# Attention and FFN in one kernel: one key transpose for each pair of heads, and the order of the cast loads

## The chip, the cores and the metric

The kernel runs on one core of a Trainium2 chip. The metric is the device time of one execution in microseconds, the median of several runs. The engines are PE (matmul; its weight loads are listed apart as PEld), DVE (vector), ACT (activations), POOL (general purpose) and SP (here only a queue that issues DMAs). They work side by side, each in the order of its own queue, and wait for each other on semaphores. DMAs run on 16 DMA engines which all queues share.

## The reference

Attention with queries pooled by two, for 8 batches of 8 heads of 1,152 positions of 64 values, then a feed-forward part without an activation function:

```python
q_pool = q.reshape(B, H, S // 2, 2, D).mean(axis=3)          # 576 queries a head
scores = np.matmul(q_pool, k.transpose(0, 1, 3, 2)) / np.sqrt(D)
attn = np.exp(scores - np.max(scores, axis=-1, keepdims=True))
attn = attn / (np.sum(attn, axis=-1, keepdims=True) + 1e-09)
attn_out = np.matmul(attn, v)
x = attn_out.transpose(0, 2, 1, 3).reshape(B * S // 2, H * D)   # 4608 x 512
out = ((x @ w1) * (x @ w2) @ w3) @ w_out
```

Inputs and output are float32. The kernel works in float16 with sums in float32, and multiplies w3 and w_out into one matrix first.

## The kernel before

**Tiles.** Two heads of one batch make a *pair*; there are 32 pairs (P = 0 to 31), and four of them make a batch. Of a pair, q, k and v are loaded by POOL-issued DMAs that cast float32 to float16 on the way, into `qst` (shared by an even and the next odd pair, 2 buffers), `kst` and `vst` (4 buffers each). The keys are needed transposed (`kT`, 64 values of two heads on 128 partitions, 9 blocks of 128 keys), and so are the pooled queries (`qT`).

**Two ways of transposing.** Pairs 0 to 7 are transposed on PE. From pair 8 on, `prep_dma(P)` does two pairs in one round. On POOL it adds neighbouring queries (`pool_q`, L122) and copies the keys of each pair from `kst` into `kc`, heads side by side (L142). On SP it issues a DMA transpose of the keys of both pairs, 18 blocks in one instruction (L145), and one of the pooled queries of both, 9 blocks (L148). There is one `kc` buffer for two pairs, and two of `kT` and of `qT`, again for two pairs each.

**The round's end.** Straight after `prep_dma`, `settled` (L152) has POOL copy one element of `kT`, so that POOL stands until the key transpose has landed. Then `load_two` (L106) issues six cast loads for the two pairs after: q, q, v, v, k, k. POOL does nothing else in this part of the program, so its instructions form one serial chain: q add, two key copies, the wait, six loads, and again. There are 12 rounds (pairs 8, 10, ... 30); the last one issues no loads.

**The main loop** (L576) has 108 iterations of three score chunks of 512 columns each. `scores` (L292) multiplies `kT` with `qT` on PE, `expo` (L302) takes the exponential on ACT into a ring, `attend` (L317) multiplies with V (`vt`, copied from `vst` on DVE, L135), and `normalize` divides on DVE and sends the result through DMA transposes on SP into `xT` (L342, L345). FFN units of 512 tokens (L411, L429) are put between these on PE once their batch is there. The loop is written out by hand (`manual_schedule`): each engine's queue has the order in which the program names the instructions. `prep_dma(P)` stands where the scores have reached 1.95 pairs ahead of pair P, but POOL isn't paced by that place: it runs as its own waits let it.

**Waits around the change.** A key transpose waits until PE has done the scores of the two pairs that held its `kT` buffer (for the round of pair P, pairs P-4 and P-3). A V load waits for the DVE copy out of its `vst` buffer. SP's queue also holds the `xT` transposes and the output writes (L450), in the program's order.

Of the kernel before, what the change touches and what calls it, by code (L numbers as in the profile page):

```python
# [23 lines left out]
def kernel(  # L24
# [11 lines left out]
    nc = tc.nc  # L36
# [38 lines left out]
    kst, vst, qst, kT, qT, kTs, qTs, qps = {}, {}, {}, {}, {}, {}, {}, {}  # L75

    def load_q(P):
        b, h0 = P // 4, 2 * (P % 4)
        if P % 2 == 0 or P == 1:
            qst[P // 2] = stage.tile([128, 2, 18, D], FP16, tag="qst", bufs=2, name="qst")  # L80
        o = 64 * (P % 2)
        nc.gpsimd.dma_start(
            out=qst[P // 2][o:o + 64].rearrange("p u t d -> p u (t d)"),
            in_=q[b, h0:h0 + 2].rearrange("u (p t) d -> p u (t d)", t=18))

    def load_k(P):
        b, h0 = P // 4, 2 * (P % 4)
        kst[P] = stage.tile([128, 2, NJ, D], FP16, tag="kst", name="kst")
        nc.gpsimd.dma_start(  # L89
            out=kst[P].rearrange("p u j d -> p u (j d)"),  # L90
            in_=k[b, h0:h0 + 2].rearrange("u (p j) d -> p u (j d)", j=NJ))

    def load_v(P):
        b, h0 = P // 4, 2 * (P % 4)
        vst[P] = stage.tile([128, 2, NJ, D], FP16, tag="vst", name="vst")
        nc.gpsimd.dma_start(  # L96
            out=vst[P].rearrange("p u j d -> p u (j d)"),
            in_=v[b, h0:h0 + 2].rearrange("u (p j) d -> p u (j d)", j=NJ))
# [7 lines left out]
    def load_two(P):  # L106
        load_q(P)
        load_q(P + 1)
        load_v(P)
        load_v(P + 1)  # L110
        load_k(P)
        load_k(P + 1)

    def pool_q(P, n=1):

        eng = nc.gpsimd if n == 2 else nc.vector
        pp, o = P // 2, 64 * (P % 2)
        if P % 2 == 0 or P == 1:
            qps[pp] = ab.tile([128, NJ, 2, D], FP16, tag="qp", bufs=2, name="qp")
        r = slice(o, o + 64 * n)  # L120
        src = qst[pp][r].rearrange("p u (c two) d -> p u c two d", two=2)
        eng.tensor_tensor(  # L122
            out=qps[pp][r].rearrange("p c u d -> p u c d"),
            in0=src[:, :, :, 0, :], in1=src[:, :, :, 1, :], op=ALU.add)

    def new_kq(P):
        if P % 2 == 0:
            kTs[P // 2] = ab.tile([128, 2, NJ, 128], FP16, tag="kT", bufs=2, name="kT")
            qTs[P // 2] = ab.tile([128, NJ, 128], FP16, tag="qT", bufs=2, name="qT")
        o = 64 * (P % 2)  # L130
        kT[P] = kTs[P // 2][:, P % 2]
        qT[P] = qTs[P // 2][:, :, o:o + 64]
# [4 lines left out]
    def prep_dma(P):  # L137

        pool_q(P, 2)
        for p in (P, P + 1):  # L140
            new_kq(p)
            nc.gpsimd.tensor_copy(  # L142
                out=new_kc(p).rearrange("p j u d -> p u j d").bitcast(mybir.dt.int32),
                in_=kst.pop(p).bitcast(mybir.dt.int32))
        nc.sync.dma_start_transpose(  # L145
            out=kTs[P // 2].rearrange("p t j f -> p (t j) f"),
            in_=kc2[P // 2].rearrange("p t j u d -> p (t j u d)"))
        nc.sync.dma_start_transpose(  # L148
            out=qTs[P // 2], in_=qps[P // 2].rearrange("p c u d -> p (c u d)"))

    def settled(P):
        nc.gpsimd.tensor_copy(out=seen, in_=kT[P][0:1, 0, 0:1])  # L152
# [1 line left out]
    kcs, kc2 = {}, {}  # L154

    def new_kc(P):
        if P % 2 == 0:
            kc2[P // 2] = ab.tile([128, 2, NJ, 2, D], FP16, tag="kc", bufs=1, name="kc")
        kcs[P] = kc2[P // 2][:, P % 2]
        return kcs[P]  # L160
# [241 lines left out]
    def ffn_groups(t):  # L402
# [70 lines left out]
        out=ident, in_=ident, compare_op=ALU.not_equal, fill=1.0,  # L473
# [102 lines left out]
    for it in range(NIT):  # L576
# [23 lines left out]
        if prepped < NPE:  # L600
            if it >= first_it(prepped) - (1 if prepped < 5 else 2):
                queue[0:0] = prep_groups(prepped)
                prepped += 1
                urgent = True
        elif prepped < NP and at >= prepped - 1.95:
            prep_dma(prepped)
            if loaded < NP:
                settled(prepped)
                load_two(loaded)
                loaded += 2  # L610
            prepped += 2
# [65 lines left out]
```

## Time and profile before

| what | value |
|---|---|
| median of 5 runs | 422.16 us |
| the five runs | 418.27, 420.03, 422.16, 423.85, 425.68 us |
| the profiled execution (one of the five) | 418.27 us |
| its span in the trace | 416.5 us |
| mean granted PE clock | 1.00 |
| POOL's queue (loads that cast) | 32.97 MB, 51.1% of 16 DMA engines |
| SP's queue (transposes, output) | 25.84 MB, 33.4% of 16 DMA engines |
| key transpose L145 | 12 times, 2.69 us of SP each, landing after 4.7 us (median) |
| query transpose L148 | 12 times, 1.37 us of SP each, landing after 4.3 us (median) |
| loads to landing (median): q, V, k | 6.4, 9.3, 11.4 us |

The span is what the trace covers; the profiled execution's own time is 1.8 us longer. A busy share is an average over the whole span. A line of a timeline has start, duration, engine, line of the kernel, the operation with what it writes and reads, and in brackets the idle time before it and what ended it. A line of the waits names who waited for whom, then the total, the number of times and the longest, in us.

### The profile page before, as it was taken

The page shows a single profiled execution, that of the slowest core. Times are in us where ns is not written, and L with a number is a line of the kernel's source. Part 1 is how long each engine was busy: PE and PEld are TensorE (multiplying, and loading weights), DVE is VectorE, ACT ScalarE, POOL GpSimd, SP SyncE. Part 2 cuts the span into 40 slices and gives each one's busy share as a digit, 9 for nine tenths or more (in the row PEclk, how much of TensorE's full clock was granted, in tenths as well). Part 3 has the DMA queues.
Part 4 walks back from the last instruction along what each step waited for, and adds up shares of the span by engine and source line. Part 5 has one row for each costly group of instructions (what it writes and reads, how often), then busy time and mean ns, then how long its engine had stood idle before and what let it go on. Part 6 is the DMA issues. An engine that isn't in the chain of part 4 may idle for free.

```text
span 416.5 us, 12709 instructions
## 1 busy us (share of the span) xinstructions
PE 406.3 (98%) x5507; PEld 271.7 (65%) x5507; DVE 195.7 (47%) x407; ACT 326.8 (78%) x357; POOL 121.0 (29%) x161
## 2 busy tenths in 40 slices
PE   8899999999999999999999999999999999999996
PEld 6677787766776577666865686667665876544443
DVE  2456655464445553555455534544455434614140
ACT  5999989989888889988888899898888889133332
POOL 6443331343435243434233161615252000000000
PEclk9999999999999999999999999999999999999999
DMA  8999999599989999997989998999898641050404
GB/s 185 204 200 193 192 205 203 104 171 136 175 154 207 141 149 168 168 170 132 164 131 210 120 175 165 181 130 162 174 186 145 97 90 22 10 117 2 102 2 102
DMA packets 95801, 59.76 MB, mean 143 GB/s; under 512 B 65152, under 2 KB 86144, under 8 KB 95744
## 3 DMA queue, kind: packets, MB, share of 16 engines
q0 software_dynamic: 26928, 32.97, 51.1%
q1 hardware_dynamic: 68656, 25.84, 33.4%
q8 instruction: 43, 0.70, 0.7%
q10 hardware_dynamic: 160, 0.13, 0.1%
q14 instruction: 14, 0.11, 0.1%
HBM read 67.11 MB, written 9.44 MB: 184 GB/s over the span
## 4 chain that ended last, share of the span: by engine, by line
PE 84%; DMA 10%; ACT 2%; POOL 1%; DVE 1%; issue 1%; SPq 0%; ACTq 0%; POOLq 0%
PE po L317 19%; PE psc L292 17%; PE pa L411 16%; PE pb L411 15%; PE pp L429 15%; DMA qst<-in_q_dram 7%; DMA xT<-in_moe_w_out_dram 3%; ACT er L302 2%; PE pT L395 2%; DMA out_dram<-osb 1%; DMA er<-in_k_dram 1%; POOL kst L89 0%; POOL w3h L356 0%; POOL vst L96 0%; DVE qp L122 0%
## 5 line engine op out<-in xcount | busy, mean ns | idle before, releaser
L302 ACT ACTIVATE er<-psc 128x1024 f16<-128x1024 f32 x324 | 307.4, 1029 | 39.7 <-PE psc L292 39.6
L317 PEld LDWEIGHTS <-er 128*128 128x128 f16 x2880 | 103.3, 97 | 22.0 <-issue 5.9
L317 PE MATMUL po<-vt,er 128*128 128x65 f16 x2880 | 110.3, 193 | 0.0
L292 PE MATMUL psc<-qT,kT 64*128 64x512 f16 (+7 forms) x1152 | 94.9, 285 | 3.0 <-ACT er L302 2.3
L423 DVE TENSOR_TENSOR gT<-pb,asb 128x512 f16<-128x512 f32 x72 | 49.8, 692 | 56.1 <-PE pb L411 55.4
L411 PE MATMUL pa<-xT,w1sb 128*128 128x512 f16 x288 | 74.2, 380 | 0.0
L411 PE MATMUL pb<-xT,w2sb 128*128 128x512 f16 x288 | 74.1, 380 | 0.0
L429 PE MATMUL pp<-T,gT 128*128 128x256 f16 (+1 forms) x488 | 67.9, 292 | 0.0
L292 PEld LDWEIGHTS <-kT 64*128 64x128 f16 x1152 | 45.6, 94 | 26.4 <-issue 6.5
L429 PEld LDWEIGHTS <-gT 128*128 128x128 f16 x488 | 45.7, 98 | 18.5 <-issue 3.7
L421 DVE COPY asb<-pa 128x512 f32<-128x512 f32 x56 | 38.7, 691 | 40.0 <-PE pa L411 38.9
L411 PEld LDWEIGHTS <-w2sb 128*128 128x128 f16 x288 | 26.4, 98 | 32.7 <-issue 3.9
L411 PEld LDWEIGHTS <-w1sb 128*128 128x128 f16 x288 | 25.0, 98 | 30.1 <-issue 6.2
L122 POOL TENSOR_TENSOR qp<-qst 128x1152 f16<-128x1152 f16 x12 | 28.5, 2379 | 45.8 <-DMA qst<-in_q_dram 24.9
L441 DVE TENSOR_SCALAR osb<-pp 128x256 f32<-128x256 f32 x49 | 20.8, 425 | 39.3 <-PE pp L429 32.6
L330 DVE RECIPROCAL rz<-po 128x5 f32<-128x5 f32 x64 | 12.4, 194 | 48.6 <-PE po L317 48.2
L334 DVE TENSOR_TENSOR xn<-po,rz 128x320 f16<-128x320 f32 x64 | 31.4, 491 | 2.5 <-DVE rz L330 0.3
L142 POOL COPY kc<-kst 128x576 int32<-128x576 int32 x24 | 15.9, 664 | 52.4 <-DMA kst<-in_k_dram 52.4
L96 POOL DMA_DIRECT2D vst<-in_v_dram x32 | 23.4, 741 | 13.7 <-DMA w3h<-in_moe_w_dram 4.2
L438 ACT ACTIVATE osb<-pp 128x512 f32<-128x512 f32 (+1 forms) x12 | 7.0, 579 | 24.0 <-PE pp L429 20.4
L89 POOL DMA_DIRECT2D kst<-in_k_dram x31 | 22.6, 743 | 9.1 <-DMA w1sb<-in_moe_w_dram 2.1
L419 ACT COPY asb<-pa 128x512 f32<-128x512 f32 x16 | 9.4, 585 | 16.5 <-PE pa L411 16.5
(42 smaller groups left out, 149.1 us busy)
## 6 DMA issues: line engine op xcount, KB each, us to landing
vst<-in_v_dram POOLq DMA_DIRECT2D x32, 288.0 KB, 9.3
out_dram<-osb SPq DMA_DIRECT2D x70, 128.0 KB, 3.7
kst<-in_k_dram POOLq DMA_DIRECT2D x31, 288.0 KB, 11.4
qst<-in_q_dram POOLq DMA_DIRECT2D x31, 288.0 KB, 6.4
w3h<-in_moe_w_dram POOLq DMA_DIRECT2D x3, 512.0 KB, 14.9
xT<-in_moe_w_out_dram POOLq DMA_DIRECT2D x4, 256.0 KB, 11.1
w1sb<-in_moe_w_dram POOLq DMA_DIRECT2D x2, 512.0 KB, 16.3
w2sb<-in_moe_w_dram POOLq DMA_DIRECT2D x2, 512.0 KB, 16.4
```

The lines of the kernel that those rows point to most:

```text
L89: nc.gpsimd.dma_start(out=kst[P].rearrange("p u j d -> p u (j d)"), in_=k[b, h0:h0 + 2].rearrange("u (p j) d -> p u (j d)", j=NJ))
L96: nc.gpsimd.dma_start(out=vst[P].rearrange("p u j d -> p u (j d)"), in_=v[b, h0:h0 + 2].rearrange("u (p j) d -> p u (j d)", j=NJ))
L122: eng.tensor_tensor(out=qps[pp][r].rearrange("p c u d -> p u c d"), in0=src[:, :, :, 0, :], in1=src[:, :, :, 1, :], op=ALU.add)
L292: nc.tensor.matmul(t[:, u, o:o + ln].rearrange("p (c f) -> p c f", f=64), kT[P][s, j, :], qT[P][s, f0 // 64:(f0 + ln) // 64], start=True, ...
L302: nc.scalar.activation(out=er[:, :, r:r + CH], in_=psc.pop(c), func=AF.Exp, bias=0.0, scale=SCALE)
L317: nc.tensor.matmul(po[P, u][:, VW * x:VW * x + D + 1], er[:, u, r:r + 128], vts[P % 4][:, u, j, 0:D + 1], start=(m == 0), stop=(m == 44), ...
L334: nc.vector.tensor_tensor(out=xn[:, P % 2, :, u, :], in0=acc[:, :, 0:D], in1=rz.to_broadcast([128, 5, D]), op=ALU.mult)
L411: nc.tensor.matmul(p, w[:, mc, ft * 128:ft * 128 + 128], xT[:, mc, t0:t0 + 512], start=(mc == 0), stop=(mc == NC - 1))
L421: nc.vector.tensor_copy(out=asb[ft], in_=p)
L423: nc.vector.tensor_mul(out=gT[:, ft, :], in0=p, in1=asb.pop(ft))
L429: nc.tensor.matmul(p[:, 0:n], gT[:, ft, 128 * i:128 * i + 128], T16[:, ft, n * s:n * s + n], start=(ft == 0), stop=(ft == NF - 1))
L441: nc.vector.tensor_scalar_mul(out=osb, in0=p[:, 0:n], scalar1=1.0 / (SCL * SCL))
```

## The change

Three edits. `load_two` issues the first pair's keys ahead of both V, and the second pair's keys last, as before. `prep_dma` issues one key transpose of 9 blocks for each pair instead of one of 18, with the query transpose between the two. And as `settled` reads only `kT[P]` of the first pair, and that is now written by a transpose of its own, POOL's wait is for that transpose alone. No line of `settled` changes.

```diff
     def load_two(P):
         load_q(P)
         load_q(P + 1)
+        load_k(P)
         load_v(P)
         load_v(P + 1)
-        load_k(P)
         load_k(P + 1)
...
-        nc.sync.dma_start_transpose(
-            out=kTs[P // 2].rearrange("p t j f -> p (t j) f"),
-            in_=kc2[P // 2].rearrange("p t j u d -> p (t j u d)"))
-        nc.sync.dma_start_transpose(
-            out=qTs[P // 2], in_=qps[P // 2].rearrange("p c u d -> p (c u d)"))
+        for p in (P, P + 1):
+            nc.sync.dma_start_transpose(
+                out=kT[p], in_=kcs[p].rearrange("p j u d -> p (j u d)"))
+            if p == P:
+                nc.sync.dma_start_transpose(
+                    out=qTs[P // 2], in_=qps[P // 2].rearrange("p c u d -> p (c u d)"))
 
     def settled(P):
         nc.gpsimd.tensor_copy(out=seen, in_=kT[P][0:1, 0, 0:1])
```

## The prediction

> **What bounds the kernel now.** I read the page's head first, then the engine table of stretches, the list of waits, and last the timelines of POOL and SP.
>
> ```profile
> PE 406.3 (98%) x5507; PEld 271.7 (65%) x5507; DVE 195.7 (47%) x407; ACT 326.8 (78%) x357; POOL 121.0 (29%) x161
> PE   8899999999999999999999999999999999999996
> DMA  8999999599989999997989998999898641050404
> 86.00:356.00 270.00, 269.98 (x3879) 183.12 (x3876) 132.23 (x271) 234.52 (x247) 88.19 (x110) 1.00 0.92 150
> ```
>
> The last line is the stretch in which the changed code runs (columns: length, busy PE, PEld, DVE, ACT, POOL, clock, DMA share, GB/s). PE shows 269.98 of 270.00 us at clock 1.00. In all 416.5 us I find 5.0 us between PE's rows, all the larger ones (0.25 to 0.82) before 75 us. So in this execution nothing that the change touches delays PE by more than a trace. DMA is the second resource, at 0.92.
>
> ```profile
> POOL seen L152 <- DMA kT<-kc: 57.0, 11, 6.7
> POOL kc L142 <- DMA kst<-in_k_dram: 52.4, 22, 5.1
> POOL qp L122 <- DMA qst<-in_q_dram: 24.9, 7, 4.4
> ```
>
> These are POOL's longest waits (total, times, longest). POOL runs a serial loop, one round for two pairs: add q, copy the keys of each pair, wait for the key transpose, issue six loads. One round of it, then the transposes of the same round on SP:
>
> ```profile
> 96.18 2.35 POOL L122 TENSOR_TENSOR qp<-qst 128x1152 f16<-128x1152 f16 x1 [4.41 <-DMA qst<-in_q_dram]
> 99.89 0.66 POOL L142 COPY kc<-kst 128x576 int32<-128x576 int32 x1 [1.36 <-DMA kst<-in_k_dram]
> 101.22 0.67 POOL L142 COPY kc<-kst 128x576 int32<-128x576 int32 x1 [0.67 <-DMA kst<-in_k_dram]
> 106.72 0.18 POOL L152 COPY seen<-kT 1x1 f16<-1x1 f16 x1 [4.83 <-DMA kT<-kc]
> 101.91 2.74 SPq L145 DMA_TRANSPOSE kT<-kc  x1
> 104.70 1.37 SPq L148 DMA_TRANSPOSE qT<-qp  x1
> ```
>
> To see whether POOL's waits matter I set landings against use. The q transpose of pairs 8 and 9 lands at 85.10+3.4 = 88.5, and pair 8's first score matmul starts at 89.67; pairs 10 and 11 land at 104.70+4.0 = 108.7 against 109.35 (each pair has 36 of the 1,152 score matmuls, so every 36th starts a pair). The slack is 1.2 and 0.65 us. Later rounds have 2.7 to 6. The loop's period from 106.7 to 303.0 is 196.3/9 = 21.8 us, PE's for two pairs 22.3 (109.35 to 310.24, nine rounds). **PE bounds this execution, but a DMA loop runs less than 1 us behind at its closest.**
>
> **What the Trainium skill says.** "DMA: Bandwidth & Descriptors", Queues, rings and completion order: each DMA engine takes turns between the queues that have work, packet by packet. So a transpose issued while casts run shares its engines. The trace agrees: K alone lands in 4.6 to 4.7 us mostly (6.5 twice); xT transposes took a median of 4.7 near 87 and 10.0 near 131, the latter under load. The same page's Rules for kernel authors say that a transpose beside ordinary DMAs needs no serializing; the trace already has the q transpose overlapping the casts (landing 3.3 to 5.0). "Perfetto Trace Analysis", Tensor Engine Instruction: matmul ends are estimated. So I rest the claim that PE is the bound also on the repeat of the schedule: pairs 10, 18 and 26 start at 109.35, 198.11, 286.53, steps of 88.76 and 88.42, so DMA jitter can hold at most about 0.35 us of each.
>
> **The change, part by part.** All times against this execution.
>
> *Split transpose.* L145's 12 instructions of 18 blocks (2.69 us of SP) become 24 of 9. The q transpose also has 9 blocks, and takes 1.37, so two cost 2.74: SP +0.05 a round, 0.6 in all, beside PE. In the built order K of the first pair waits only for the first copy's count, q follows it, and the second K waits for the second copy. SP may stand at that second K with xT (L342) and output writes behind it; before, it stood at the joint K until the same copy, so they come at most 0.05 later. xT has room: the last xT of batches 1 to 3 is issued at 108.8, 151.3, 197.0, its FFN unit starts at 123.1, 165.95, 209.1 (12 us or more; landings up to 10).
>
> *Round of pair 8.* The copies start at 81.09, the first ends at 81.7. First K then issues at 81.7 instead of 82.37, q at 83.1 instead of 85.10, and q lands at 86.5: 2 us more slack. First K lands with q's shortest 3.3, at 85.1, where the joint one landed at 87.07. POOL's wait ends there and the loads start 2.0 us earlier, at 85.7.
>
> *K of the first pair ahead of both V.* In the next round the first K load landed at 99.85 after two V; in third place it should land where the first V did (88.88+8.0 = 96.9), 3 us earlier, and with the earlier start at 95. The q add ends at 96.5, the copy at 97.2, and first K transposes while V and the second K still load. q's transpose issues at 98.5 and lands near 102.6 (108.7 before). The second K is copied at about 99.9. First K, under load, lands at 100.5 to 102.2, so the next loads start 4.5 to 6 us earlier than 107.18. Then each round would win some 4 us more (4.8 of wait down to 1) until the release of kT holds: round P's K waits for the scores of pair P-3. Before, K issued 9 to 12.6 us after that, so the lead stops at some 10 us.
>
> V moves back one place, about 2 us, but starts 2 us earlier in the first round: v of pair 10 lands at 97, its copy on DVE is at 102.35. 5 us stay, later more. V loads wait for DVE copies made some 16 us before, so a 10 us lead still fits.
>
> *What is added.* The odd pair's first score waits for its own K: 12 more waits on PE. The waits that PE's queue shows at this line take 51 ns: 0.6 us at most; as they ride on weight loads, I take 0. Whether the second K is slow under load the trace doesn't show for certain. Below: 3.3 us (q's best); above: 16.8 (the longest V landing). In the first round it is issued at 84.5 and pair 9 starts at 99.29: 14.8 us, nothing lost up to there. I take 8, lost 0.
>
> Sum on the profiled execution: 418.27 (span 416.5 and 1.8 around) less 0 to 0.7 of stalls, plus 0 to 0.6: **418.2**. The median of the five is 422.16, the highest 425.68. The profiled one is the lowest. So the question is what the other 3.9 us are. Two places depend on DMA: the first 78 us (share 1.2 at 195 to 202 GB/s, and 17.2 us of the chain are one wait for a q load; not touched here) and the loop. Of a loop period of 21.8 us, POOL's own work is 2.35+0.66+0.67, so 83% is waiting for DMA. A DMA slower by 3% costs the first place some 0.03x47 = 1.4 (its q landing at 47.1 ends the DMA part of the chain); the loop, from 82.4 to pair 26's q at 280.4+3.4, some 0.03x201x0.83 = 5.0, less 2.7 of slack there, or 2.3. The sum is 3.7, about the difference to the median, and the loop has 62% of it (68% at 4%). I take 65%; this estimate rests on the spread being DMA at all. Removing that: 422.16 - 0.65x3.9 = **419.6**.
>
> **The rivals.**
> 1. All the spread comes from the loop: then every run falls to PE's own time, 417.3. For: the slack of 0.65. Against: DMA is fuller still before 78 us.
> 2. Nothing of the spread is the loop (the early loads, or PE's clock in the other runs): 422. For: the profiled execution shows no stall. The change then does what it says, POOL's wait falls, and no time follows.
> 3. Slower: second K shares its engines with six casts and is late for the odd pair. It decides once a landing takes over 13 to 15 us; at 14.8+0.5 us, all 12 odd pairs stall half a microsecond, 428 from the median. Against: the lead grows after the first round, and no transpose here took over 10 by its median.
> 4. The copies or V loads still hold first K, so that the loop stays at 21.8: as rival 2. The built waits speak against it.
>
> **How the numbers follow.** Forecast 0.42 (418.2 to 421.5), rival 1 0.26, rivals 2 and 4 0.22, rival 3 0.10. About 1% can be told from no change, so faster means below 417.9 and slower above 426.4. Faster: most of rival 1 and a little of the forecast, 0.28. Slower: rival 3 and the upper end of rival 2, 0.11. The rest, 0.61, is within. The range 416.5 to 424.5 takes the forecast, nearly all of rival 1 and most of 2.
>
> **What would show it.** POOL's wait at the seen copy falls from 57.0 us to below 25; the first loads start near 85.7; the q transpose of pair 10 issues near 98.5, 6 us earlier; later rounds lead by about 10 us; PE stays at 269.9 of 270 between 86 and 356. Wrong: a PE wait for kT at an odd pair, or at an FFN unit for xT; a loop period still at 21.8 with no lead; or runs that keep a spread of 7 us, which would put that spread elsewhere.

## The result

| | before | changed |
|---|---|---|
| median | 421.96 us (52 runs) | 419.27 us (31 runs) |
| lowest to highest | 417.69 to 429.73 us | 418.1 to 420.76 us |
| profiled execution, its span | 418.27, 416.5 us | 418.67, 416.9 us |

The ratio is 0.9954, with a 95% interval of 0.9936 to 0.9971: 0.46% faster, which is real and below the 1% bound. Ratios, here and below, leave out runs more than 1.5% above their kernel's fastest, while medians and ranges hold all; in the kernel before those runs are part of the spread in question, so the ratio understates the gain (by the medians it is 0.64%). The lowest time didn't fall. What changed is the spread: from the lowest to the highest run, 12.0 us became 2.7 us, and the middle half of the runs, 3.8 us wide before, is 0.7 us wide.

The profile after repeats what the profile before showed of PE. First the same stretch in the changed kernel (length, busy PE, PEld, DVE, ACT, POOL, clock, DMA share, GB/s), then POOL's longest waits:

```profile
86.00:356.00 270.00, 269.98 (x3877) 183.16 (x3874) 134.02 (x271) 234.48 (x247) 87.12 (x108) 1.00 0.96 149
```
```profile
POOL kc L142 <- DMA kst<-in_k_dram: 50.0, 11, 5.7
POOL seen L153 <- DMA kT<-kc: 45.1, 11, 10.7
POOL qp L122 <- DMA qst<-in_q_dram: 24.2, 5, 11.0
```

PE is as full in both, so the two profiled executions can't show the gain: the one of before was among that kernel's fastest. At the seen copy POOL waits 45.1 us where it was 57.0, but its idle time ahead of the q add for which no releaser is seen grew from 10.4 to 22.6; with the keys and q, the sum is 141.9 us for 144.7. So POOL's idle time moved more than it fell. The round of pair 10 on POOL, then on SP:

```profile
95.85 0.66 POOL L142 COPY kc<-kst 128x576 int32<-128x576 int32 x1 [1.34 <-issue]
100.61 0.67 POOL L142 COPY kc<-kst 128x576 int32<-128x576 int32 x1 [4.10 <-DMA kst<-in_k_dram]
103.22 0.18 POOL L153 COPY seen<-kT 1x1 f16<-1x1 f16 x1 [1.95 <-DMA kT<-kc]
```
```profile
96.54 1.43 SPq L146 DMA_TRANSPOSE kT<-kc  x1
98.02 2.57 SPq L149 DMA_TRANSPOSE qT<-qp  x1
101.30 1.78 SPq L146 DMA_TRANSPOSE kT<-kc  x1
```

The first key transpose is issued between the two copies, and the query transpose follows at 98.02 where it stood at 104.70. It lands 5.9 us later, at 103.9; pair 10's scores start at 109.31. The 0.6 us of slack has become 5.4.

### The profile page after: what moved, and what is told of

Same layout as the page of the kernel before. It is cut to its first block, busy times and chain, and to the rows that moved or that the text cites. A ratio compares the mean times of both kernels' runs of the same rounds, so it can differ in the third digit from the quotient of the medians.

```text
span 416.9 us, 12736 instructions
## 1 busy us (share of the span) xinstructions
PE 406.4 (97%) x5507; PEld 271.6 (65%) x5507; DVE 197.5 (47%) x407; ACT 326.7 (78%) x357; POOL 120.7 (29%) x161
## 4 chain that ended last, share of the span: by engine, by line
PE 88%; ACT 5%; DMA 3%; issue 1%; DVE 1%; POOL 1%; SPq 0%; ACTq 0%
PE po L318 20%; PE psc L293 19%; PE pa L412 16%; PE pb L412 15%; PE pp L430 15%; ACT er L303 5%; PE pT L396 3%; DMA qst<-in_q_dram 2%; DMA out_dram<-osb 1%; DMA er<-in_k_dram 1%; PE t L170 0%; PE w3t L384 0%; POOL vst L96 0%; DVE qp L122 0%; POOL kst L89 0%
## 5 line engine op out<-in xcount | busy, mean ns | idle before, releaser
L331 DVE RECIPROCAL rz<-po 128x5 f32<-128x5 f32 x64 | 12.4, 194 | 48.1 <-PE po L318 47.7
L96 POOL DMA_DIRECT2D vst<-in_v_dram x32 | 23.4, 744 | 12.0 <-DMA w3h<-in_moe_w_dram 4.4
## 6 DMA issues: line engine op xcount, KB each, us to landing
kst<-in_k_dram POOLq DMA_DIRECT2D x31, 288.0 KB, 11.2
xT<-in_moe_w_out_dram POOLq DMA_DIRECT2D x4, 256.0 KB, 10.3
```

The source lines that it names most:

```text
L96: nc.gpsimd.dma_start(out=vst[P].rearrange("p u j d -> p u (j d)"), in_=v[b, h0:h0 + 2].rearrange("u (p j) d -> p u (j d)", j=NJ))
```

## The experiments

Theory 1 is that of the prediction: POOL's DMA loop is late for PE in most executions of the kernel before, though not in the profiled one. Theory 2 says that the spread comes from elsewhere, PE's clock or the early loads. Each ratio below is against runs of the kernel before on the same chip (median 421.5 to 422.5); the range is of all runs, and some kernels have few.

| kernel | median (runs), us | lowest to highest | ratio, 95% interval |
|---|---|---|---|
| `b_again`: before, unchanged | 422.28 (22) | 418.28 to 426.72 | 0.9992, 0.9965 to 1.0019 |
| `order_only` | 421.99 (22) | 417.66 to 425.74 | 0.9996, 0.9970 to 1.0023 |
| `split_only` | 419.15 (10) | 418.16 to 421.16 | 0.9927, 0.9898 to 0.9955 |
| `split_second` | 418.87 (20) | 418.09 to 420.95 | 0.9943, 0.9923 to 0.9964 |
| `wait_second` | 418.66 (8) | 418.23 to 420.87 | 0.9911, 0.9878 to 0.9943 |
| `q_first` | 417.94 (6) | 417.68 to 418.19 | 0.9902, 0.9864 to 0.9939 |
| `q_split` | 418.80 (7) | 418.38 to 420.11 | 0.9929, 0.9900 to 0.9958 |
| `before_extra` | 435.32 (4) | 431.99 to 438.88 | 1.0342, 1.0276 to 1.0408 |
| `after_extra` | 418.65 (14) | 417.92 to 420.67 | 0.9934, 0.9908 to 0.9959 |
| `q_first_extra` | 424.85 (12) | 419.80 to 427.11 | 1.0071, 1.0030 to 1.0112 |
| `before_nowait` | 435.91 (6) | 432.28 to 440.47 | 1.0247, 1.0191 to 1.0303 |
| `after_nowait` | 427.93 (4) | 427.23 to 429.01 | 1.0141, 1.0100 to 1.0182 |

### Another profile of the kernel before

No edit.

> The kernel before, unchanged, to see the granted clock and the span of each of its runs and another profile. Theory 1 (the DMA loop of POOL is late for PE in most executions): median near 422, spread 418 to 427, with slow runs at clock 0.995 or more, and a profile of an execution above 420 us shows PE idle at the start of an even pair's scores (for qT or kT). Theory 2 (the spread is PE's clock or the early loads): times fall as the clock rises over the whole spread, or a slow profile shows the lost time before 80 us or spread evenly.

This time the profiled execution took 420.41 us, 2.1 us more than the first. Its stretch, PE's longest wait for a DMA in it, and PE's timeline where that wait ends:

```profile
86.00:356.00 270.00, 268.24 (x3851) 181.94 (x3848) 131.71 (x269) 233.20 (x246) 88.26 (x110) 1.00 0.94 149
```
```profile
PE psc L292 <- DMA qT<-qp: 1.6, 2, 1.1
```
```profile
286.24 0.66 PE L292 MATMUL psc<-qT,kT 64*128 64x512 f16 x8
288.05 0.34 PE L292 MATMUL psc<-qT,kT 64*128 64x384 f16 x2 [1.15 <-DMA qT<-qp]
```

That is the wait that the first profile didn't have: the first scores of pair 26 stand until the query transpose lands. Setting landing against use for all rounds, as the prediction did, gives the slack of q in us, to about 0.1:

| scores of pair | 10 | 14 | 18 | 22 | 26 | 30 |
|---|---|---|---|---|---|---|
| before, 418.27 us | 0.6 | 5.0 | 3.4 | 4.4 | 2.7 | 6.1 |
| before again, 420.41 us | 1.5 | 3.4 | 0.1 | 0.0 | 0.0 | 0.0 |
| changed, 418.67 us | 5.4 | 12.7 | 12.1 | 17.8 | 14.1 | 17.8 |
| `q_first`, 418.02 us | 5.7 | 10.5 | 11.9 | 16.3 | 15.2 | 19.2 |

The slack of 0.0 means that the scores start as q lands, so the loop leads. From the first to the eleventh of POOL's seen copies a round took 22.3 us on average (86.78 to 309.73), and 21.6 in the first profile (87.14 to 303.04); PE needs 22.3. From pair 8's first scores to pair 31's it took 255.4 us here and 253.1 there: 2.2 us, all of the difference, is lost in the loop's stretch. This speaks for theory 1. The stalls are at pairs 18, 26 and 30, not at pair 10, where the first profile had its 0.6 us: what decides is that the rounds grew longer.

One part of the expectation didn't come. The runs of `b_again` above 422.5 us had mean clocks of 0.992 to 0.996, and those below 420.5 us 0.998 to 1.000: the sign that had been named for theory 2. Whether the clock is cause or effect there this profile, at clock 1.00, can't tell; `q_first` below bears on it. It is one execution at 420.41; those at 425 weren't seen in a trace.

### Which part of the change does it

`order_only` is the changed `load_two` in the kernel before:

```diff
         load_q(P + 1)
+        load_k(P)
         load_v(P)
         load_v(P + 1)
-        load_k(P)
         load_k(P + 1)
```

> Only the load order: first pair's keys ahead of both V, one joint key transpose of 18 blocks, POOL waits for it whole. The joint transpose still needs the second key copy, which comes last. Theory 1: the loop keeps its period of 21.8 us, so nothing is gained: 421 to 422.5, spread as before. Theory 2: no part of the change matters much by itself, 420 to 422. If this alone gives 419.3, V's place in the queue is what counts and not the transpose.

421.99, ratio 0.9996: nothing, as expected. The joint transpose still needs the second copy.

`split_only` is the changed `prep_dma` with the old load order:

> Only the split: one transpose for each pair, POOL waits for the first, but loads in the old order q, q, v, v, k, k. First K starts after the first key copy, some 1.4 us before the second, and is half as long: the loop is 2 us a round shorter. Theory 1: 2 us a round is enough (a slack of 0.65 at pair 10 becomes about 4.5, then more), so nearly the whole gain: 419.3 to 420, spread under 4 us. Theory 2: as order_only, 420 to 422.

419.15: the whole gain. Its q slack is 3.6 at pair 10 and 10.3 at pair 18. The earlier load isn't needed for it.

`wait_second` and `split_second` take away the third part, the wait for the first transpose alone, in the changed kernel and in `split_only`:

```diff
-        nc.gpsimd.tensor_copy(out=seen, in_=kT[P][0:1, 0, 0:1])
+        nc.gpsimd.tensor_copy(out=seen, in_=kT[P + 1][0:1, 0, 0:1])
```

> The changed kernel, but POOL's copy of one element reads kT of the second pair, so that the loads wait for the second transpose. The order of loads and both transposes stay. First K and q are still early, by about 6 us from pair 10 on, but the loads start 2 to 5 us later a round than in the changed kernel. Theory 1: q's slack is 5 or more from pair 10 on at a period near 21, so most of the gain stays: 419.3 to 420.5. If the early loads are what counts: 421 to 422.

> Split transposes, q between them, loads in the old order, and POOL waits for the second K. What is left of the change is that first K and q are issued after the first key copy and 1.4 us sooner behind a half as long K. If slack at q's landing is the cause: 418.5 to 419.5, as with the whole change. If the earlier start of the loads is: 421 to 422.

418.66 and 418.87. So neither the order nor the wait for the first alone is worth anything that these runs can tell; the split alone carries the gain. What is left in `split_second` is an earlier query transpose, behind half the keys and after one copy. Its q slack is 4.4 at pair 10 and never under 7 from pair 12 on.

### Only the landing of q

`q_first` leaves the joint transpose, the old order and the wait as they were, and swaps two statements:

```diff
+        nc.sync.dma_start_transpose(
+            out=qTs[P // 2], in_=qps[P // 2].rearrange("p c u d -> p (c u d)"))
         nc.sync.dma_start_transpose(
             out=kTs[P // 2].rearrange("p t j f -> p (t j) f"),
             in_=kc2[P // 2].rearrange("p t j u d -> p (t j u d)"))
-        nc.sync.dma_start_transpose(
-            out=qTs[P // 2], in_=qps[P // 2].rearrange("p c u d -> p (c u d)"))
```

> The kernel before with the query transpose issued ahead of the joint key transpose. q no longer waits for the key copies, so it lands some 7 us earlier, and K becomes the last to land, at the same time as before: 2.7 us ahead of use at pairs 8 and 10 in place of 0.6 to 1.2. The loop's period stays near 21.8. Theory 1a (what matters is any slack at the landing): stalls such as the 2.0 us in the second profile of the kernel before go, 419.5 to 420.5, but the highest runs stay above 422. Theory 1b (only a shorter period helps): 421.5 to 422.5.

SP in the round of pair 10:

```profile
96.09 1.40 SPq L145 DMA_TRANSPOSE qT<-qp  x1
101.34 2.69 SPq L147 DMA_TRANSPOSE kT<-kc  x1
```

417.94, and all six runs within 0.5 us: better than the 419.5 to 420.5 expected, and no run above 422 was left. q had been queued on SP behind keys that it doesn't depend on. POOL's round still takes 21.2 us (86.82 to 298.35, ten rounds). In the profile of `order_only` it takes as long (85.89 to 298.21), and that kernel's median stayed at 421.99. So this speaks for the slack at the landing, and not for a shorter loop, as what ends the stalls here; both profiles are of executions near their kernel's fastest. The clocks of the six runs were 0.998 to 1.000, where the runs of the kernel before on the same chip had a median of 0.996. K is now last, about 2.8 us ahead of pair 10 (101.34+4.7 against 108.84).

`q_split` does the same in the changed kernel:

> The changed kernel with its query transpose issued ahead of the first pair's keys instead of between the two. Slack at q and at K both, and the short loop: 417.7 to 418.5, as q_first (417.94) or a trace better, and below the changed kernel (419.27). If the changed kernel's last 1.3 us over q_first come from its transposes running beside the loads: 418.7 to 419.3, as before this edit.

418.80, the second of the two cases: no better than the change. The profiled executions (418.80 and 418.02) show where their difference lies. Pair 8's scores start at 89.88 us here and at 89.15 in `q_first`, so 0.73 us of it is there before the first of these rounds is used. From pair 8 to pair 31 it is 253.1 here and 253.4 there, and 74.0 and 73.7 after pair 31's start. The second difference, of 0.3 us, lies after PE's last matmul; its cause is open.

The same reading of the other profiles tells what the remaining spread is. In eight of them, from 417.66 to 419.99 us (the kernel before at 418.27, the changed one, `order_only`, `split_only`, `split_second`, `wait_second`, `q_split`, `after_extra`), the way from pair 8 to pair 31 is 253.1 us each time. What differs is pair 8's start, from 89.02 to 90.87 us. In the latest of these, `split_second`, PE stands once for 1.26 us at 14.56, where it waits for an early pair's pooled queries from DVE. So some 2 us of spread lie ahead of pair 8, where theory 2 had put the early loads, and none of these edits aims at them; the stalls of theory 1 come on top.

### How much delay each version bears

The extra load, ahead of the six in `load_two`, reads V into a tile that no one uses (the line that declares the tile is left out here):

```diff
+        nc.gpsimd.dma_start(
+            out=spin_in.rearrange("p u j d -> p u (j d)"),
+            in_=v[P // 4, 0:2].rearrange("u (p j) d -> p u (j d)", j=NJ))
         load_q(P)
```

> The kernel before with one more cast load of 288 KB a round, of V into a tile that nothing reads, ahead of the six loads. It lengthens the DMA loop by one load, some 2 us a round. Theory 1 (loop of 21.8 us just under PE's 22.3): 11 rounds at 23.8 against 22.3 are 16 us behind, less the little slack there is: 432 to 440, and PE stands before the scores of every even pair. Theory 2 (loop not decisive): DMA is beside PE, 422 to 424.

> The changed kernel with the same extra load. Theory 1: its loop runs free at 18.4 to 20.9 us a round and has to wait for PE in some rounds, so 2 us more still fit under 22.3: 419 to 422, at least 10 us under the kernel before with the same load. Theory 2: as much slower as the kernel before is with it.

> The kernel before with the query transpose ahead of the joint key transpose and the extra cast load of 288 KB a round. If q_first gained only slack at the landing, its loop is still some 21.2 us and becomes 23.2 with the load, 0.9 behind PE's 22.3 a round, 10 rounds, less 2.7 of slack: 424 to 428, between the kernel before with the load (435.3) and the changed one with it (418.7). If q_first took away the cause altogether: 418 to 420.

435.32 and 424.85 are where theory 1 put them, and 418.65 is just below its range of 419 to 422. In the kernel before with the load, q's slack is 0.1 us or less at seven of the twelve rounds, and PE waits for q for 8.0 us in all. The changed kernel takes the same load without a loss. `q_first` loses, and PE's waits there name the keys instead. The line of the kernel before with the load, then that of `q_first` with it:

```profile
PE psc L296 <- DMA qT<-qp: 8.0, 6, 3.1
PE psc L296 <- DMA kT<-kc: 7.5, 4, 3.0
```

So the change has the larger margin. The swap alone has the better median, though over six runs, and the two ratios' intervals just overlap.

### Without POOL's wait

The line `settled(prepped)` is left out:

> The kernel before without POOL's one-element copy, so the loads are issued right after the key copies, and nothing else is changed. The joint transpose then runs beside the loads. Theory 1: each round is up to 5 us shorter, less what the transposes lose beside the loads, so it does as well as the change: 419 to 420, spread below 4 us. If the wait was needed because transposes beside casts get very slow: 423 or more, with PE waiting for kT or qT.

> The changed kernel without POOL's one-element copy. The joint key transpose lost by this (14.2 us to landing beside six loads, 435.9). Here the first K is mostly done when the loads start, but q and the second K run beside them. If the wait protects q of the first round: q lands some 7 to 9 us after issue, 1 to 2 us late for pair 8, one stall and a stretch of lower clock: 420 to 426. If half transposes don't mind the loads: 418.5 to 419.5.

435.91 is a miss for theory 1's 419 to 420; the other case named there, 423 or more with PE waiting for qT or kT, came. 427.93 is beyond the 420 to 426 of its first case. PE's timeline in the first, at pair 8, and SP's before it:

```profile
89.17 0.98 PE L317 MATMUL po<-vt,er 128*128 128x65 f16 x27
99.05 1.46 PE L292 MATMUL psc<-qT,kT 64*128 64x512 f16 x10 [8.90 <-DMA qT<-qp]
```
```profile
82.31 4.40 SPq L145 DMA_TRANSPOSE kT<-kc  x1
86.76 7.19 SPq L148 DMA_TRANSPOSE qT<-qp  x1
```

The six loads start at 82.22 with the transposes. The joint key transpose takes a median of 14.2 us to landing over this kernel's rounds where it took 4.7, and the query transpose of pair 8 lands 12.2 us after its issue. In the changed kernel without the wait PE stands 7.2 us at the same place, and a half key transpose has a median of 8.1 us. So POOL's wait isn't waste: it keeps a transpose away from six loads. The change keeps most of that protection, and no transpose of keys took more than 7.9 us in it.

## Why the prediction was right

**Median and sign.** 419.6 was forecast and 419.27 measured. The step that carried it was to set the landing of q and the loop's period against PE's use, and then to ask what the runs above the profiled one are. The 0.65 us at pair 10 itself wasn't the place of the stalls in the second profile: those came at later rounds, as these had become longer. 65% of the 3.9 us was put on the loop; 421.96 to 419.27 is 2.7 us, or 69% of 3.9. That the shares agree so well is luck in part. The 3% was assumed. The 83% counts as waiting the 4.2 us a round in which POOL issues its loads; its three waits shown there sum to 134.3 us, 12.2 a round or 56%, and with 56% the same sum gives 0.03x201x0.56 - 2.7 = 0.7 us for the loop in place of 2.3. Against that, in `b_again` ten rounds took 223.0 us for 215.9, 3.3% more, and the loop's stretch lost 2.2 us, near the 2.3 forecast for 3%. But the 1.4 us that the sum gave to the early loads weren't there: pair 8 started at 89.60 us for 89.67.

**The profiled execution.** 418.2 was the sum, 418.67 came: no gain there, as said. Of the 0.40 us by which it lies above the one of before, none is in the loop (253.1 us both) nor before pair 8 (89.63 for 89.67): PE's last matmul ends at 412.38 us for 412.41, and what follows takes 0.4 us more. Its cause is open.

**The rivals.** Rival 1 (all of the spread is the loop) is nearer the truth than its 0.26: a kernel with slack at q (`q_first`) had no spread to speak of in six runs, 417.68 to 418.19, though its early loads are the same. It isn't the whole truth: the other kernels' profiles differ by up to 1.85 us ahead of pair 8. Rival 2 is out as the main cause by `q_first` and by the extra loads, which touch neither the early loads nor PE's clock directly; `b_again`'s profile agrees. Rival 3 didn't happen: the second K landed 3.3 to 5.3 us after issue and at least 10 us ahead of its pair. Its premise, that a transpose suffers beside casts, is true at a size that I had argued against with "no transpose here took over 10 by its median": without the wait it is 14.2. The landings of xT had been read too kindly as well: in the profile of before they go up to 12.4 us, not 10, and the median of 4.7 near 87 us is the middle of only two, 2.5 and 7.0, of which the second already ran beside casts.

**Split transpose.** Right in kind: q 2 us earlier at pair 8 was the estimate; its slack there went from 1.2 to 3.5. The SP cost was mis-sized: q's instruction took a median of 1.55 and up to 3.18 us instead of 1.37, now that it is issued while loads run. It lies beside PE.

**First pair's keys ahead of V.** Here the working credited a step that doesn't matter. The first copy did come earlier (10.5 us after the round's loads start, 12.2 before), but the runs show no time from it, and the round didn't win "some 4 us more". With first K and q under load (first K landed after 6.6 us at pair 10, not 3.3 to 5), the second keys' load was no earlier (copied 15.3 us after the round's loads start, 13.6 before). The loads after it started at 103.68, 3.5 us earlier than 107.18 and not 4.5 to 6. From pair 8's seen copy on, three rounds took 18.4, 19.3 and 19.7 us where the kernel before took 19.6, 20.0 and 23.4: 1.9 less on the mean, not 4.

**POOL's wait.** Forecast below 25 us, measured 45.1. Three of the eleven waits, 7.7, 10.7 and 7.2, make 25.6 of it: there POOL had run ahead. At pair 16 SP was still issuing output writes before the first key transpose:

```profile
155.63 4.29 SPq L451 DMA_DIRECT2D out_dram<-osb  x4
160.03 1.33 SPq L146 DMA_TRANSPOSE kT<-kc  x1
```

kT had been free since pair 14's scores began at 155.80. The other two waits, at pairs 24 and 28, look the same: output writes to 247.8 and 290.6, then the transpose 0.1 us later, with kT free 3.4 and 4.2 us before. So the lead ended at SP's program order there, where I had named the release of kT. The other eight waits have 2.4 us on average, not 1. The size of the lead fits: q's slack is 12 to 18 us from pair 14 on, where some 10 was said.

**What was added.** The 12 extra PE waits cost nothing visible: PE is busy 269.98 us in both.

## What to carry to other kernels

A profile of one of the fastest executions can show a full engine and no wait, and still hide what sets the median. Compare the profiled time with the runs, and list the slack of each landing against its first use. Here a slack under 1 us in a serial DMA loop, whose period was within 3% of the engine's, went with stalls in other executions, at other rounds than the one with the least slack. Comparing the same stretch of several profiles (253.1 us for pairs 8 to 31) then tells which part of a difference belongs to the change. Before splitting or reordering transfers, look for one that is queued behind something it doesn't depend on; here the swap of two statements did as much for the median as the change. A wait that looks idle may keep a transfer out of a crowd, so test it by taking it away before counting it as gain.

## What was not expected of the hardware

PE's granted clock fell to half after some of its stalls. In the kernel before without POOL's wait it was granted 0.50 from 92.2 to 102.5 us, with work again from 99.05 on (columns as above):

```profile
92.20:102.50 10.30, 3.45 (x21) 1.52 (x22) 0.13 (x1) 2.74 (x3) 5.64 (x8) 0.50 1.05 155
102.50:110.00 7.50, 7.50 (x141) 5.26 (x139) 3.77 (x8) 5.62 (x7) 0.95 (x2) 1.00 1.21 170
```

Pair 8 took 11.2 us to pair 9 there, instead of 9.6: some 1.6 us lost on top of the stall of 8.9. With the extra load, PE's wait of 2.14 us for q before 345.10 was followed by half clock from 346.1 for 3.4 us. But waits of 3.0 us in `q_first_extra` and 1.15 in `b_again`, and one of 3.06 at 201.1 in the same profile as the 2.14, left the clock at 1.00. The Trainium skill, "TensorE: Matmul & The Clock Gate", Part 1: The HAM clock gate, states that PE's clock is halved after an idle window of about 3.4 us and that the window runs free of the kernel. The lengths agree with such a step (3.41 us, and 10.24, three of it); the 2.14 us that sufficed once is less than the page's window, and the measurement decides: what else must come together isn't shown. So a late landing can cost more than its wait, and a lower mean clock in a run may be the effect of a stall and not the cause of the time: on one chip the median over the runs was 0.996 in the kernel before, 0.988 with the extra load, and 0.9995 in `q_first`, which differs by the order of two DMA instructions. So in these runs the order of DMAs moved the clock along with the time. In the highest runs of the kernel before the stall and the half clock weren't traced, and how much of their time is the one or the other stays open.
